# LN1 of tiles 6 to 15 transposed by DMA instead of TensorE, normalised three tiles ahead, with the weight loads behind the transposes

## The chip, the core and the metric

The kernel runs on one core of one Trainium2 chip. The metric is the device time of one execution in microseconds (us). Inside the core five engines follow their own instruction streams in order and meet at semaphores: TensorE (PE, with its weight loads shown apart as PEld), VectorE (DVE), ScalarE (ACT), GpSimd (POOL) and SyncE (SP). In this kernel SP issues all DMAs, so its stream is also the order of the one DMA queue.

## The reference

One transformer block of 2048 tokens and width 512 in bf16, with linear attention of 32 heads of 16 columns and a feed-forward part of width 1792:

```
x  = A_x                                   # 2048 x 512
q, k, v = split(layernorm(x) @ wqkv)       # 32 heads of 16
phi(t) = where(t > 0, t + 1, exp(t)) + 1e-6
kv = sum_s phi(k)[s] v[s]^T ;  z = sum_s phi(k)[s]
o  = phi(q) kv / (phi(q) . z + 1e-6)
h  = x + o @ wo
out = h + relu(layernorm(h) @ w1) @ w2
```

`B_x` is not used. The layernorms have no weights.

## The kernel before

The 2048 rows are 16 tiles of 128 rows (`NT`), and four chunks of four tiles (`CT`, 512 rows). The weights and all of x stay in SBUF. No scheduler orders the work (`manual_schedule`): each engine executes its instructions in the order in which the Python code issues them, and the semaphores alone are set automatically.

The kernel has two parts. **The key loop** (lines 313 to 330) goes over the 16 tiles and is what the change touches. **The rest** (from line 333) computes z, the small matrices of the heads and wo, the queries, h, the second layernorm and the feed-forward part, chunk by chunk. The second layernorm of chunks 1 to 3 is transposed by DMA already (`ln2_norm`, line 452).

In the key loop a tile t goes through these steps; the short names are the code's:

- `A_S(t)`, here **S(t)**: DVE takes the statistics of x (`st`, line 175, and `mv`, line 176). When the group of t is complete, ACT computes 1/sqrt(var + eps) as a Ln and an Exp (`rstd`, lines 169 and 170). Tiles 0 to 3 are groups of one, and the others are pairs: (4, 5), (6, 7), (8, 9) and so on. S of an odd tile is thus followed by the two small ACT instructions, and the norms of both tiles wait for them.
- `A_N(t)`, here **N(t)**: DVE writes the normalised tile `ln` (line 179).
- `A_T(t)`, here **T(t)**: four TensorE transposes of 128x128 into PSUM (line 187), and one ACT copy to `lnT` (line 193).
- `A_K(t)`, here **K(t)**: four matmuls, `lnT` by the key weights into `kps` (line 294).
- `phi_act(t)`: ACT reads `kps` and writes `e` = exp (line 199), and for some tiles also `r` = relu (line 203).
- `phi_dve(t)`: DVE clips `e` (line 208) and then adds, as `r + e` where ACT made the relu (`pk_all`, line 212), or as max(kps, 0) + e straight from PSUM where it did not (line 214).
- `A_G(t)`, here **G(t)**: four matmuls, `ln` by `pk_all`, accumulate the 512x512 matrix `gps` (line 301).

Iteration i issues T(i+1), K(i), G(i-1), phi_act(i), N(i+2), S(i+4), phi_dve(i), with S(3) and S(4), S(5) in iterations 0 and 1. TensorE thus repeats transposes, K and G, 12 instructions an iteration, and G(i-1) is the one that needs what DVE made last. Iterations 14 and 15 also hold a group of four query matmuls each (`q_group`, line 326), which need `wq_sb`.

SP issues x and the key weights first (lines 83 to 92), and then `wq`, `wv`, `wo`, `w1` and `w2` as five whole loads (lines 93 to 97). All of that is issued in the first 13.0 us, and SP's next work are the transposes of line 452. The first use of `wq` is at 36.7 us, of `wv` at 45.3 us, of `wo` at 48.1 us, and of `w1` at 61.9 us.

Of the kernel before, what the change touches and what calls it, by code (L numbers as in the profile page):

```python
# [11 lines left out]
BF16 = mybir.dt.bfloat16  # L12
# [4 lines left out]
def kernel(  # L17
# [13 lines left out]
    nc = tc.nc  # L31
    P = 128
    xf = A_x.flatten_outer_dims()
    of = out.flatten_outer_dims()
    S, D = xf.shape
# [3 lines left out]
    NT = S // P  # L39
    CW = 512  # L40
    CT = CW // P
# [6 lines left out]
    work = ctx.enter_context(tc.tile_pool(name="work", bufs=2))  # L48
# [7 lines left out]
    wqkv_v = A_wqkv.rearrange("(k p) n -> p k n", p=P)  # L56

    x_nat = big.tile([P, NT, D], BF16, name="x_nat")
    wq_sb = const.tile([P, KD, D], BF16, name="wq_sb")
    wk_sb = const.tile([P, KD, D], BF16, name="wk_sb")  # L60
    wv_sb = const.tile([P, KD, D], BF16, name="wv_sb")
    wo_sb = const.tile([P, KD, D], BF16, name="wo_sb")
    w1_sb = const.tile([P, KD, FF], BF16, name="w1_sb")
    w2_sb = const.tile([P, KF, D], BF16, name="w2_sb")
# [3 lines left out]
        name=nc.get_next_instruction_name(),  # L68
# [6 lines left out]
    def load_x(t0, n):  # L75
        nc.sync.dma_start(out=x_nat[:, t0 : t0 + n, :], in_=x_v[:, t0 : t0 + n, :])

    def load_wk(h):
# [11 lines left out]
    load_x(6, 2)  # L90
    load_x(8, 4)
    load_x(12, 4)
    nc.sync.dma_start(out=wq_sb[:], in_=wqkv_v[:, :, 0:D])
    nc.sync.dma_start(out=wv_sb[:], in_=wqkv_v[:, :, 2 * D : 3 * D])
    nc.sync.dma_start(out=wo_sb[:], in_=A_wo.rearrange("(k p) n -> p k n", p=P))
    nc.sync.dma_start(out=w1_sb[:], in_=B_w1.rearrange("(k p) n -> p k n", p=P))
    nc.sync.dma_start(out=w2_sb[:], in_=B_w2.rearrange("(k p) n -> p k n", p=P))


    eps5 = const.tile([P, 1], F32, name="eps5")  # L100
# [13 lines left out]
        out=mask3, in_=mask3, pattern=[[-DH, P // DH], [0, DH]],  # L114
# [3 lines left out]
        out=mask3, in_=mask3, pattern=[[DH, P // DH], [0, DH]],  # L118
# [8 lines left out]
        out=mask_h[:], in_=mask_h[:], pattern=[[P, KD], [-DH, H]],  # L127
# [3 lines left out]
        out=mask_h[:], in_=mask_h[:], pattern=[[-P, KD], [DH, H]],  # L131
# [4 lines left out]
        out=erep[:], in_=erep[:], pattern=[[1, D]],  # L136
# [3 lines left out]
        out=erep[:], in_=erep[:], pattern=[[-1, D]],  # L140
# [5 lines left out]
    lnT_c = [big.tile([P, KD, CW], BF16, name=f"lnT{c}") for c in range(NCH)]  # L146
# [20 lines left out]
    def rstd_of(mv, n):  # L167
        rstd = work.tile([P, n], F32, name="rstd", tag=f"rstd{n}", bufs=4)
        nc.scalar.activation(out=rstd[:], in_=mv[:, :, 1], func=ACT.Ln, bias=eps5[:], scale=1.0)
        nc.scalar.activation(out=rstd[:], in_=rstd[:], func=ACT.Exp, scale=-0.5)  # L170
        return rstd

    def stats(mv, k, src):
        st = work.tile([P, nc.vector.BN_STATS_DIM], F32, name="st", tag="st", bufs=4)
        nc.vector.bn_stats(out=st[:], in_=src)  # L175
        nc.vector.bn_aggr(out=mv[:, k, :], in_=st[:])  # L176

    def norm(dst, src, mv, rstd, k):
        nc.vector.tensor_scalar(  # L179
            out=dst, in0=src, scalar1=mv[:, k, 0:1], scalar2=rstd[:, k : k + 1],  # L180
            op0=ALU.subtract, op1=ALU.mult,
        )
# [7 lines left out]
    def evac_T(dst3, tp, on_act, k=KD):  # L190
        src3 = tp.rearrange("p (k n) -> p k n", k=k)
        if on_act:
            nc.scalar.activation(out=dst3, in_=src3, func=ACT.Copy)  # L193
        else:
            nc.vector.tensor_copy(out=dst3, in_=src3)

    def phi_act(ps, relu_on_act):
        e = work.tile([P, CW], BF16, name="e", tag="e", bufs=4)
        nc.scalar.activation(out=e[:], in_=ps, func=ACT.Exp)  # L199
        r = None  # L200
        if relu_on_act:
            r = work.tile([P, CW], BF16, name="r", tag="r", bufs=4)
            nc.scalar.activation(out=r[:], in_=ps, func=ACT.Relu)
        return e, r

    def phi_dve(ps, dst, er):
        e, r = er
        nc.vector.tensor_scalar(  # L208
            out=e[:], in0=e[:], scalar1=1.0, scalar2=1e-6, op0=ALU.min, op1=ALU.add
        )  # L210
        if r is not None:
            nc.vector.tensor_tensor(out=dst, in0=r[:], in1=e[:], op=ALU.add)
        else:
            nc.vector.scalar_tensor_tensor(  # L214
                out=dst, in0=ps, scalar=0.0, in1=e[:], op0=ALU.max, op1=ALU.add
            )
# [16 lines left out]
    def tick():  # L233
        due = [x for x in later if x[0] <= 0]
        later[:] = [x for x in later if x[0] > 0]
        for x in later:
            x[0] -= 1
        for _, fn in due:
            fn()
# [5 lines left out]
    def q_group(c, jq, relu_on_act):  # L245
        qps = q_mm(c, jq)
        er = phi_act(qps[:], relu_on_act)
        after(0, lambda: phi_dve(qps[:], pqT_c[c][:, jq, :], er))
# [6 lines left out]
    mvs, rstds, lns, tps, kpss, ers = {}, {}, {}, {}, {}, {}  # L255

    def A_S(t):
        g, k = where[t]
        if k == 0:
            mvs[g[0]] = work.tile(  # L260
                [P, len(g), nc.vector.BN_AGGR_DIM], F32, name="mv", tag=f"mv{len(g)}", bufs=4
            )
        stats(mvs[g[0]], k, x_nat[:, t, :])
        if k == len(g) - 1:
            rstds[g[0]] = rstd_of(mvs[g[0]], len(g))

    def A_N(t):
        g, k = where[t]
        lns[t] = work.tile([P, D], BF16, name="ln", tag="ln", bufs=6)
        norm(lns[t][:], x_nat[:, t, :], mvs[g[0]], rstds[g[0]], k)  # L270

    def A_first():

        lns[0] = work.tile([P, D], BF16, name="ln", tag="ln", bufs=6)
        for k in range(0, KD, 2):
            cols = slice(k * P, (k + 2) * P)
            norm(lns[0][:, cols], x_nat[:, 0, cols], mvs[0], rstds[0], 0)
        for k in range(0, KD, 2):
            tp = psum.tile([P, 2 * P], BF16, name="tph", tag="mm")
            for i in range(2):  # L280
                nc.tensor.transpose(
                    tp[:, i * P : (i + 1) * P], lns[0][:, (k + i) * P : (k + i + 1) * P], ident[:]
                )
            evac_T(lnT_c[0][:, k : k + 2, 0:P], tp, on_act=True, k=2)

    def A_T(t):
        c, j = divmod(t, CT)
        evac_T(lnT_c[c][:, :, j * P : (j + 1) * P], transpose(lns[t]), on_act=True)

    def A_K(t):  # L290
        c, j = divmod(t, CT)
        kpss[t] = psum.tile([P, D], F32, name="kps", tag="mm")
        for kd in range(KD):
            nc.tensor.matmul(  # L294
                kpss[t][:], lhsT=lnT_c[c][:, kd, j * P : (j + 1) * P], rhs=wk_sb[:, kd, :],
                start=(kd == 0), stop=(kd == KD - 1),
            )

    def A_G(t):
        for kd in range(KD):  # L300
            nc.tensor.matmul(  # L301
                gps[kd][:], lhsT=lns[t][:, kd * P : (kd + 1) * P], rhs=pk_all[:, t, :],
                start=(t == 0), stop=(t == NT - 1),
            )

    ok = lambda t: 0 <= t < NT
    A_S(0)
    A_S(1)
    A_first()
    warm(1)  # L310
    A_N(1)
    A_S(2)
    for i in range(NT):
        if ok(i + 1):
            A_T(i + 1)
        A_K(i)
        if ok(i - 1):
            A_G(i - 1)
        ers[i] = phi_act(kpss[i][:], relu_on_act=(i % 3 != 2))
        if ok(i + 2):  # L320
            A_N(i + 2)
        t = {0: 3, 1: 4}.get(i, i + 4)
        if ok(t):
            A_S(t)
        if i >= NT - 2:
            q_group(0, i - (NT - 2), False)
        phi_dve(kpss[i][:], pk_all[:, i, :], ers[i])
        if i == 1:
            A_S(5)
        tick()  # L330


# [276 lines left out]
```

## Time and profile before

| what | us |
|---|---|
| time, median of 3 runs (182.0 to 182.14) | 182.02 |
| span of the profiled execution, first to last instruction | 180.3 |
| median time less that span | 1.7 |
| PE busy in the span | 170.8 |
| DVE busy in the span | 110.4 |
| ACT busy in the span | 80.9 |
| first K to the last G of the key loop on PE | 6.0 to 43.9 |

The profile is of one execution. Its page states the span alone and no device time of its own; the median of the runs is 1.7 us longer. A line of the timeline gives the start and the length of an instruction or of a merged row of equal ones, its engine and line, what it writes and reads, and in brackets how long the engine idled before it and what released it. A table by stage gives the busy time of each engine in a stretch of the span. Granted TensorE clock is 1.00 in every stretch of the span. A PE row ends when its last result is out of the array, so that a row of four matmuls of 512 columns shows 1.03 us, while the next row can start 0.865 us after it; starts are what can be compared.

### The profile page before, as it was taken

The numbers are of one execution on the slowest core, as the hardware profiler recorded it, in microseconds if no ns is written. First come the engines' busy times: TensorE is split into PE (matmuls) and PEld (weight loads), VectorE is DVE, ScalarE is ACT, GpSimd is POOL, SyncE is SP. The second block draws the span as 40 slices with busy tenths as digits, with TensorE's granted clock in tenths as the row PEclk, the third lists the DMA queues.
The fourth block names the chain that finished last, engine by engine and source line by source line (L and its number), as shares of the span: only waits on it lengthen the run. The fifth ranks groups of instructions, "written<-read, shape, count | busy, mean of one in ns | idle before, by whom it ended". The sixth has DMA issues, their size and how long they took to land.

```text
span 180.3 us, 2413 instructions
## 1 busy us (share of the span) xinstructions
PE 170.8 (95%) x899; PEld 80.1 (44%) x916; DVE 110.4 (61%) x247; ACT 80.9 (45%) x162; POOL 4.0 (2%) x15
## 2 busy tenths in 40 slices
PE   7778999999999999999999999999999999999992
PEld 2334555546444444444444344444444444444461
DVE  3889999556799866988223788433498713343220
ACT  3768888856674998323007722003932100332000
POOL 7100000000000000000000000000000000000000
PEclk9999999999999999999999999999999999999999
DMA  5999970000000000002410000431000250000011
GB/s 139 291 331 378 377 232 4 0 0 4 0 4 0 0 0 0 2 4 58 111 35 29 0 4 0 87 87 58 0 0 4 40 135 29 29 0 4 29 58 31
DMA packets 15627, 11.69 MB, mean 65 GB/s; under 512 B 7040, under 2 KB 15104, under 8 KB 15616
## 3 DMA queue, kind: packets, MB, share of 16 engines
q1 hardware_dynamic: 15616, 11.54, 21.1%
q8 instruction: 7, 0.11, 0.2%
q14 instruction: 4, 0.03, 0.1%
HBM read 7.86 MB, written 2.10 MB: 55 GB/s over the span
## 4 chain that ended last, share of the span: by engine, by line
PE 70%; DVE 18%; ACT 6%; issue 2%; DMA 1%; DVEq 0%
PE fps L489 22%; PE pps L475 20%; PE gps L301 7%; PE kps L294 6%; DVE st L175 5%; PE qps L221 5%; PE hps L419 5%; DVE at L482 2%; PE fpsh L489 2%; DVE hn L179 2%; DVE mv L176 2%; DVE h_nat L443 1%; ACT lden L406 1%; ACT rden L408 1%; PE tp L187 1%
## 5 line engine op out<-in xcount | busy, mean ns | idle before, releaser
L475 PE MATMUL pps<-lnT,w_sb 128*128 128x512 bf16 x220 | 53.0, 379 | 0.8 <-ACT lnT L193 0.4
L489 PE MATMUL fps<-w_sb,at 128*128 128x512 bf16 x205 | 46.1, 379 | 0.6 <-DVE at L482 0.4
L480 ACT ACTIVATE at<-pps 128x512 bf16<-128x512 f32 x28 | 16.6, 595 | 60.6 <-PE pps L475 60.6
L489 PEld LDWEIGHTS <-at 128*128 128x128 bf16 x238 | 23.1, 98 | 26.2 <-DVE at L482 1.3
L475 PEld LDWEIGHTS <-w_sb 128*128 128x128 bf16 x224 | 21.9, 98 | 27.3 <-issue 1.7
L497 DVE TENSOR_TENSOR o_t<-fps,h_nat 128x512 bf16<-128x512 f32 x15 | 10.4, 692 | 29.1 <-PE fps L489 29.1
L482 DVE TENSOR_SCALAR at<-pps 128x512 bf16<-128x512 f32 x28 | 19.0, 680 | 9.3 <-PE pps L475 9.3
L301 PE MATMUL gps<-pk_all,ln 128*128 128x512 bf16 x61 | 15.9, 379 | 1.0 <-DVE pk_all L214 0.5
L419 PE MATMUL hps<-m_sb,pqs 128*128 128x512 bf16 x63 | 16.6, 379 | 0.1
L294 PE MATMUL kps<-wk_sb,lnT 128*128 128x512 bf16 x62 | 16.3, 379 | 0.1
L221 PE MATMUL qps<-lnT,wq_sb 128*128 128x512 bf16 x62 | 15.7, 379 | 0.2
L175 DVE BATCH_NORM_STATS2 st<-x_nat 128x6 f32<-128x512 bf16 x16 | 11.0, 685 | 1.8 <-DMA x_nat<-in_A_x_dram 1.7
L208 DVE TENSOR_SCALAR e<-e 128x512 bf16<-128x512 bf16 x32 | 8.9, 278 | 4.7 <-ACT e L199 4.7
L199 ACT ACTIVATE e<-qps 128x512 bf16<-128x512 f32 x16 | 9.4, 600 | 4.6 <-PE qps L221 4.6
L175 DVE BATCH_NORM_STATS2 st<-h_nat 128x6 f32<-128x512 bf16 x16 | 11.0, 689 | 0.4
L410 DVE TENSOR_TENSOR pqs<-pqT,rden 128x512 bf16<-128x512 bf16 x12 | 5.1, 426 | 9.1 <-ACT rden L408 9.0
L199 ACT ACTIVATE e<-kps 128x512 bf16<-128x512 f32 x16 | 9.5, 595 | 2.5 <-PE kps L294 2.5
L193 ACT ACTIVATE lnT<-tp 128x512 bf16<-128x512 bf16 x17 | 10.0, 590 | 0.5 <-PE tp L187 0.5
L419 PEld LDWEIGHTS <-pqs 128*128 128x128 bf16 x64 | 6.2, 98 | 8.4 <-DVE pqs L410 1.2
L301 PEld LDWEIGHTS <-ln 128*128 128x128 bf16 x64 | 6.2, 97 | 8.5 <-issue 1.4
L221 PEld LDWEIGHTS <-wq_sb 128*128 128x128 bf16 x64 | 6.0, 98 | 7.2 <-issue 0.8
L443 DVE TENSOR_TENSOR h_nat<-hps,x_nat 128x512 bf16<-128x512 f32 x12 | 8.2, 686 | 0.9 <-PE hps L419 0.8
(72 smaller groups left out, 134.9 us busy)
## 6 DMA issues: line engine op xcount, KB each, us to landing
w_sb<-in_B_w_dram SPq DMA_DIRECT2D x2, 1792.0 KB, 14.0
out_dram<-o_t SPq DMA_DIRECT2D x15, 128.0 KB, 1.7
x_nat<-in_A_x_dram SPq DMA_DIRECT2D x2, 512.0 KB, 7.3
x_nat<-in_A_x_dram SPq DMA_DIRECT2D x4, 128.0 KB, 2.2
wk_sb<-in_A_wqkv_dram SPq DMA_DIRECT2D x2, 256.0 KB, 3.7
x_nat<-in_A_x_dram SPq DMA_DIRECT2D x2, 256.0 KB, 4.7
wq_sb<-in_A_wqkv_dram SPq DMA_DIRECT2D x1, 512.0 KB, 8.7
wv_sb<-in_A_wqkv_dram SPq DMA_DIRECT2D x1, 512.0 KB, 9.4
```

The source lines that it names most:

```text
L175: nc.vector.bn_stats(out=st[:], in_=src)
L199: nc.scalar.activation(out=e[:], in_=ps, func=ACT.Exp)
L221: nc.tensor.matmul(qps[:], lhsT=wq_sb[:, kd, jq * P : (jq + 1) * P], rhs=lnT_c[c][:, kd, :], start=(kd == 0), stop=(kd == KD - 1),)
L294: nc.tensor.matmul(kpss[t][:], lhsT=lnT_c[c][:, kd, j * P : (j + 1) * P], rhs=wk_sb[:, kd, :], start=(kd == 0), stop=(kd == KD - 1),)
L301: nc.tensor.matmul(gps[kd][:], lhsT=lns[t][:, kd * P : (kd + 1) * P], rhs=pk_all[:, t, :], start=(t == 0), stop=(t == NT - 1),)
L419: nc.tensor.matmul(hps[:], lhsT=pqss[c][jb][:, j * P : (j + 1) * P], rhs=m_sb[:, jb, :], start=(jb == 0), stop=(jb == KD - 1 and c > 0),)
L443: nc.vector.tensor_tensor(out=h_nat[:, t, :], in0=hps[:], in1=x_nat[:, t, :], op=ALU.add)
L475: nc.tensor.matmul(pps[:], lhsT=w1_sb[:, kd, f * P : (f + 1) * P], rhs=hnT_c[c][:, kd, :], start=(kd == 0), stop=(kd == KD - 1),)
L480: nc.scalar.activation(out=acts[c][:, f, :], in_=pps[:], func=ACT.Relu)
L482: nc.vector.tensor_scalar(out=acts[c][:, f, :], in0=pps[:], scalar1=0.0, scalar2=None, op0=ALU.max)
L489: nc.tensor.matmul(fps[:], lhsT=acts[c][:, f, j * P : (j + 1) * P], rhs=w2_sb[:, f, n0:n1], start=(f == 0), stop=(f == KF - 1),)
L497: nc.vector.tensor_tensor(out=o_t[:], in0=fps[:], in1=h_nat[:, t, n0:n1], op=ALU.add)
```

## The change

- T(6) to T(15) are gone from TensorE, and with each the ACT copy to `lnT`. In their place N(t) is followed by one DMA transpose from SBUF to SBUF, which SP issues.
- The loads of `wq`, `wv` and `wo` are cut into halves of two of four row blocks. One half is issued behind each of the transposes 6 to 11. `w1` and `w2` are issued whole behind transpose 15.
- From iteration 5 on, N is three tiles ahead (it was two) and S five tiles ahead (it was four). The catching up is in iteration 4, which issues N(6), N(7), S(8), phi_dve(4), S(9), in this order. Iterations 0 to 3 are as before, and so are the transposes on TensorE up to T(5), in iteration 4.
- ACT computes the relu of all tiles except 2 (before, DVE did it from PSUM for 2, 5, 8, 11 and 14).
- `ln` has 8 buffers (it had 6).

The rest of the kernel is not changed.

```diff
-    nc.sync.dma_start(out=wq_sb[:], in_=wqkv_v[:, :, 0:D])
-    nc.sync.dma_start(out=wv_sb[:], in_=wqkv_v[:, :, 2 * D : 3 * D])
-    nc.sync.dma_start(out=wo_sb[:], in_=A_wo.rearrange("(k p) n -> p k n", p=P))
-    nc.sync.dma_start(out=w1_sb[:], in_=B_w1.rearrange("(k p) n -> p k n", p=P))
-    nc.sync.dma_start(out=w2_sb[:], in_=B_w2.rearrange("(k p) n -> p k n", p=P))
+    wo_v = A_wo.rearrange("(k p) n -> p k n", p=P)
+    w1_v = B_w1.rearrange("(k p) n -> p k n", p=P)
+    w2_v = B_w2.rearrange("(k p) n -> p k n", p=P)
+
+    def load_half(dst, src, h):
+        nc.sync.dma_start(out=dst[:, 2 * h : 2 * h + 2, :], in_=src[:, 2 * h : 2 * h + 2, :])
+
+    wq_v, wv_v = wqkv_v[:, :, 0:D], wqkv_v[:, :, 2 * D : 3 * D]
...
+    TD = 6
+    beside = {6: (wq_sb, wq_v, 0), 7: (wq_sb, wq_v, 1), 8: (wv_sb, wv_v, 0), 9: (wv_sb, wv_v, 1),
+              10: (wo_sb, wo_v, 0), 11: (wo_sb, wo_v, 1)}
+
     def A_N(t):
         g, k = where[t]
-        lns[t] = work.tile([P, D], BF16, name="ln", tag="ln", bufs=6)
+        lns[t] = work.tile([P, D], BF16, name="ln", tag="ln", bufs=8)
         norm(lns[t][:], x_nat[:, t, :], mvs[g[0]], rstds[g[0]], k)
+        if t >= TD:
+            c, j = divmod(t, CT)
+            nc.sync.dma_start_transpose(out=lnT_c[c][:, :, j * P : (j + 1) * P], in_=lns[t][:])
+            if t in beside:
+                load_half(*beside[t])
+            if t == NT - 1:
+                nc.sync.dma_start(out=w1_sb[:], in_=w1_v)
+                nc.sync.dma_start(out=w2_sb[:], in_=w2_v)
...
+    S_at = {0: [3], 1: [4, 5], 2: [6], 3: [7], 4: [8, 9]}
+    N_at = {0: [2], 1: [3], 2: [4], 3: [5], 4: [6, 7]}
...
     for i in range(NT):
-        if ok(i + 1):
+        if ok(i + 1) and i + 1 < TD:
             A_T(i + 1)
         A_K(i)
         if ok(i - 1):
             A_G(i - 1)
-        ers[i] = phi_act(kpss[i][:], relu_on_act=(i % 3 != 2))
-        if ok(i + 2):
-            A_N(i + 2)
-        t = {0: 3, 1: 4}.get(i, i + 4)
-        if ok(t):
+        ers[i] = phi_act(kpss[i][:], relu_on_act=(i != 2))
+        for t in N_at.get(i, [i + 3]):
+            if ok(t):
+                A_N(t)
+        ss = [t for t in S_at.get(i, [i + 5]) if ok(t)]
+        for t in ss[:1]:
             A_S(t)
         if i >= NT - 2:
             q_group(0, i - (NT - 2), False)
         phi_dve(kpss[i][:], pk_all[:, i, :], ers[i])
-        if i == 1:
-            A_S(5)
+        for t in ss[1:]:
+            A_S(t)
         tick()
```

More of the change, by code (lines that the diff above doesn't have):

```diff
@@ L265, in A_S @@
             rstds[g[0]] = rstd_of(mvs[g[0]], len(g))
+    TD = 6
+    beside = {6: (wq_sb, wq_v, 0), 7: (wq_sb, wq_v, 1), 8: (wv_sb, wv_v, 0), 9: (wv_sb, wv_v, 1),
+              10: (wo_sb, wo_v, 0), 11: (wo_sb, wo_v, 1)}
     def A_N(t):
         g, k = where[t]
-        lns[t] = work.tile([P, D], BF16, name="ln", tag="ln", bufs=6)
+        lns[t] = work.tile([P, D], BF16, name="ln", tag="ln", bufs=8)
         norm(lns[t][:], x_nat[:, t, :], mvs[g[0]], rstds[g[0]], k)
+        if t >= TD:
[6 more added lines that the diff above has]
+                nc.sync.dma_start(out=w2_sb[:], in_=w2_v)
     def A_first():
-        lns[0] = work.tile([P, D], BF16, name="ln", tag="ln", bufs=6)
+        lns[0] = work.tile([P, D], BF16, name="ln", tag="ln", bufs=8)
         for k in range(0, KD, 2):
```

## The prediction, made before the changed kernel was run

> **What bounds the kernel now.** I read the page first, then the key loop, the only stage that the change touches, by a table of one row per iteration, then VectorE's timeline.
>
> ```profile
> span 180.3 us, 2413 instructions
> PE 170.8 (95%) x899; PEld 80.1 (44%) x916; DVE 110.4 (61%) x247; ACT 80.9 (45%) x162; POOL 4.0 (2%) x15
> ```
>
> The page says TensorE (PE), at 95%, and VectorE (DVE) at 61%. That is an average. In the key loop, with the stretches cut at the starts of G (so 18.52 is the start of G(4), 20.47 of G(5)), and the columns PE, weight loads, DVE, ACT:
>
> ```profile
> 16.57:18.52 1.95, 1.95 (x13) 1.00 (x12) 1.76 (x6) 1.88 (x4) 0.00 (x0) 1.00 1.02 401
> 18.52:20.47 1.95, 1.95 (x13) 1.00 (x12) 1.88 (x6) 1.54 (x4) 0.00 (x0) 1.00 1.03 395
> 28.30:30.25 1.95, 1.95 (x14) 1.01 (x13) 1.77 (x6) 1.88 (x4) 0.00 (x0) 1.00 0.00 0
> ```
>
> PE is never free here, and DVE is nearly full too: its remaining 0.1 to 0.2 us are mostly the gaps between dependent instructions, as the timeline of one iteration shows:
>
> ```profile
> 16.34 0.41 DVE L179 TENSOR_SCALAR ln<-x_nat,mv,rstd 128x512 bf16<-128x512 bf16 x1
> 16.66 0.68 DVE L175 BATCH_NORM_STATS2 st<-x_nat 128x6 f32<-128x512 bf16 x1
> 17.38 0.18 DVE L176 BATCH_NORM_AGGREGATE mv<-st 128x2 f32<-128x6 f32 x1
> 17.48 0.26 DVE L208 TENSOR_SCALAR e<-e 128x512 bf16<-128x512 bf16 x1
> 17.89 0.42 DVE L212 TENSOR_TENSOR pk_all<-r,e 128x512 bf16<-128x512 bf16 x1 [0.15 <-ACT r L203]
> 18.23 0.41 DVE L179 TENSOR_SCALAR ln<-x_nat,mv,rstd 128x512 bf16<-128x512 bf16 x1
> ```
>
> From start to start: N to S 0.32, `st` to `mv` 0.72, `mv` to `e` 0.10, `e` to `pk_all` 0.36 (15.63 to 15.99 one iteration earlier; here 0.41, held up by ACT), `pk_all` to the next N 0.35. The sum is **1.85 us**, where ACT makes the relu. Where DVE makes it (tile 5: `e` 19.38, `pk_all` 19.68, next N 20.29) the last two terms are 0.30 and 0.61 in place of 0.36 and 0.35, so 2.05. PE needs 1.95 for transposes, K and G. DVE is therefore the next bound, 0.1 us behind the present one. The rows to price the change from:
>
> ```profile
> L187 PE MATMUL tp<-ident,ln 128*128 128x128 bf16 x60 | 5.8, 219 | 1.1 <-DVE ln L179 1.1
> lnT<-hn SPq DMA_TRANSPOSE x12, 2.4
> wk_sb<-in_A_wqkv_dram SPq DMA_DIRECT2D x2, 256.0 KB, 3.7
> 81.89 5.23 SPq L452 DMA_TRANSPOSE lnT<-hn  x4
> 11.65 0.18 DVE L176 BATCH_NORM_AGGREGATE mv<-st 128x2 f32<-128x6 f32 x1
> 12.44 0.41 DVE L179 TENSOR_SCALAR ln<-x_nat,mv,rstd 128x512 bf16<-128x512 bf16 x1 [0.60 <-ACT rstd L170]
> ```
>
> **What the change takes from PE.** In the chain of waits four transposes of a tile take 0.222 us, and K and G 0.865 each: 1.95. Ten tiles lose them: 10 x 0.222 = 2.2 us of PE, if PE stays the bound at 1.73 an iteration. It does not.
>
> **A floor between K and G.** From the end of K(12)'s row (33.28 + 1.03 = 34.31) to the end of `pk_all` (35.47 + 0.42) are 1.58 us (exp, relu, add); G starts 0.05 later. K(i+1) starts 0.865 after G(i-1), its row lasts 1.03, and G(i+1) starts 1.63 behind it: 3.52 us for two iterations, 1.76 each. That is the pace where DVE is not the bound.
>
> **What DVE has to do, tile by tile.** Up to `pk_all` of tile 3 (start 15.99) the order is unchanged, and nothing there waits for a load but the first tile. From there, in the new order of DVE:
>
> - Iteration 4, N(6) N(7) S(8) phi(4): 0.35 to N(6), 0.33 to N(7) (estimate: the two `hn` norms at 57.30 take 0.70 together, 0.41 one), 0.32, 0.72, 0.10, 0.36 = 2.18. `pk_all` of 4 at 18.17, done 18.59, G(4) at **18.64** (18.52 before).
> - Then S(9), then N(8), which now needs the rstd of S(9) at once: **a new wait**. The row at 12.44 is its like: `mv` at 11.65, the Ln and Exp on ACT, N 0.79 later, with DVE idle for 0.60. On ACT the Ln stands ahead of the exp of tile 5, so that exp is held too, but it is done in time (about 20.5, and its relu 21.0). Sum: 0.34 to S(9), 0.72, 0.79 to N(8), 0.32 to S(10), 0.72, 0.10, 0.36 = 3.35. `pk_all` of 5 at 21.52, G(5) at **21.99** (20.47 before, so 1.52 late).
> - Iterations 6 to 10 hold N, S and phi each: 5 x 1.85 = 9.25. Here S of an odd tile comes before a phi, so its rstd has 0.81 us before the next N, against 0.79 needed: no further wait. `pk_all` of 10 at 30.77, G(10) at 30.77 + 0.42 + 0.05 = **31.24** (30.25 before, 0.99 late).
> - From iteration 11 on S is finished, and PE and the floor set the pace: G(11) 31.24 + 1.73 = 32.97; G(12) by the floor from K(12), which starts 31.24 + 0.865 = 32.105: 32.105 + 1.03 + 1.63 = 34.76; G(13) 36.49. Before, G(13) is at 36.10, so **0.39 us late**. Neither kernel has a T behind that, so from here the rest shifts as it is.
>
> The relus on ACT are in this sum: tiles 5 and 8 save DVE 0.20 each (2.05 to 1.85); 11 and 14 lie where DVE has time. ACT takes four relus of 0.59, and loses ten copies of 0.59 (line 193), so nothing there is late.
>
> **The transposes.** The issue takes SP 5.23 / 4 = 1.3 us, and a tile lands 2.4 us after its issue begins. A half load costs SP 0.48 (the halves of `wk`, 0.96 for two). A pair takes 1.78, less than DVE's 1.85, so SP follows N. SP is idle from 13.0 us to 81.9 before, so no other work waits behind. Transpose 6 starts with the end of N(6) at 16.8 and lands at 19.2; K(6) can start at 19.5. That is the tightest; were it late by up to 1.6 us, G(5) waits for DVE until 21.99 anyway. Transpose 7 starts at 18.6, lands at 21.0 (K(7) at 22.9); 9 at 22.3, 24.7 (K(9) 26.6); 11 at 26.0, 28.4 (K(11) 30.3). If each also waits for the half load ahead of it, add 0.7 us (256 KB at the 355 to 401 GB/s of the table's last column), which stays inside. I take no cost. The outer bound is 3.7 us for a half (the row of `wk`, which landed in a full queue): a pair of 1.2 + 3.7 = 4.9 from 16.8 lands transpose 11 at 16.8 + 5 x 4.9 + 2.4 = 43.7, 13.4 us late. The point from which it decides is a pair of 2.2 us. I choose the small end, as the new queue is nearly empty, like that of the row at 81.89.
>
> A rule speaks against this edit: the Trainium skill, VectorE: DVE Perf Modes, "The three transpose paths", gives 1309 ns to a 128x128 DMA transpose, 390 ns to one on TensorE, and advises TensorE where PSUM will do. An estimate from that page, four blocks in sequence, would be 5.2 us a tile, pairs of 5.7, and K(11) some 20 us late; the row above has all four blocks landed in 2.4.
>
> **The loads.** By the starts above, `wq` is issued by 20.4, `wv` by 24.1, `wo` by 27.8, `w1` and `w2` from about 34.5. Their uses are at 36.7, 45.3, 48.1, 61.9 and later, and `w1` and `w2` took 14.0 us: 48.5. All hidden; without that cover `w1` would have to be over 13 us later still. The 8 `ln` buffers suffice: tile t lives from N in iteration t-3 to G in t+1.
>
> **Sum.** 180.3 + 0.39 = 180.7 us of span; with the 1.7 outside, 182.02 + 0.39 = **182.4 us**, +0.21%. The measurement tells about 0.2% from no change, 0.36 us, so I stand at that edge.
>
> **The rivals.**
>
> - *PE keeps what it is given.* If the DVE group runs in 1.73 or less in place of 1.85 and the wait ahead of N(8) is filled, 2.2 us go: 179.8. For it: PE is busy in all of each iteration today, which the page shows and DVE's 61% does not contradict. Against: three cycles of 1.85 with nothing to wait for. It decides from a group under 1.76 us. Chance 0.10, with what lies on the way to it (179.8 to 181.6): faster.
> - *The wait ahead of N(8) costs nothing* (0.69 less in the sum, 0.79 against 0.10): 181.7; from 181.66 to 182.1. For it: the rstd needs two small instructions only. Against: the row at 12.44 with 0.60 idle. Chance 0.13: within 0.2%.
> - *The transposes are late*, as the half loads share their queue: a pair of 3 us would land transpose 11 at 34.2, 3.9 us late, 186.3; a pair of 2.3 some 0.5 us more than the forecast, 182.9. Chance 0.12, slower. For it: up to 3.7 us in the row of `wk`.
> - *The stretch costs DVE more*, by a second wait for rstd in iterations 7 and 9 (spare 0.02 us; up to 0.3 each): 182.8 to 183.4. Chance 0.10, slower.
> - *Forecast*, 182.1 to 182.8: chance 0.55, of which 0.33 lies above 182.38 (slower) and 0.22 below (within).
>
> Faster 0.10; within 0.13 + 0.22 = 0.35; slower 0.33 + 0.10 + 0.12 = 0.55. The range 181.4 to 183.8 leaves out most of the first rival and half of the third. It doesn't hold the outer bound of the transposes.
>
> **What would show it.** DVE idle for about 0.6 us ahead of N(8), released by ACT `rstd`; starts of G from 5 to 10 spaced at 1.85, with PE waiting for `pk_all` line by line; G(13) some 0.4 us later than at 36.10; no K waiting for a DMA but at most K(6); the rest after the loop unchanged in length. I am wrong if PE waits for `lnT` from a DMA beyond K(6), or if G comes at 1.73 to 1.76 before iteration 10.

## The result and the profile after

| kernel | median us (range) | span of the profiled execution |
|---|---|---|
| before | 182.08 (182.0 to 182.31, 4 runs) | 180.3 |
| after | 183.16 (183.0 to 183.35, 4 runs) | 181.2 |

The ratio is 1.0058, with a 95% interval of 1.0045 to 1.007: **slower by 1.1 us**. The forecast was 182.4, 0.4 slower. Direction and range hold; the size does not, and it is wrong in three terms of which two nearly cancel.

The page after, its span and its line of engines:

```profile
span 181.2 us, 2356 instructions
PE 169.8 (94%) x860; PEld 77.7 (43%) x876; DVE 109.6 (61%) x247; ACT 77.2 (43%) x156; POOL 4.0 (2%) x15
```

PE has 39 matmuls fewer in the records (40 were taken out), and is busy for 1.0 us less. (By the starts it has 2.2 us less to do, but a row that is followed by a wait counts its full 1.03 us.) The span is 0.8 longer. So PE waits more, and the table by iteration, cut at the new starts of G, says where. G(4) starts at 18.71, G(5) at 22.07, G(6) at 24.33 and so on; the columns are the length, PE, weight loads, DVE, ACT, POOL, clock, DMA share and GB/s:

```profile
18.71:22.07 3.36, 1.89 (x8) 0.77 (x8) 2.58 (x8) 2.45 (x6) 0.00 (x0) 1.00 0.58 144
22.07:24.33 2.26, 1.89 (x9) 0.78 (x8) 1.71 (x6) 0.84 (x3) 0.00 (x0) 1.00 0.87 238
24.33:26.75 2.42, 1.90 (x9) 0.70 (x9) 2.28 (x7) 0.75 (x2) 0.00 (x0) 1.00 0.67 88
...
30.47:32.32 1.85, 1.85 (x9) 0.78 (x8) 1.71 (x6) 1.51 (x4) 0.00 (x0) 1.00 0.77 202
```

Against the predicted lengths of 3.35, 1.85, 1.85 and 1.85 the first and the last hold, and two rows are too long: 2.26 (0.41 over) and 2.42 (0.57 over). DVE's timeline shows the first of these:

```profile
19.30 0.18 DVE L179 BATCH_NORM_AGGREGATE mv<-st 128x2 f32<-128x6 f32 x1
20.08 0.41 DVE L182 TENSOR_SCALAR ln<-x_nat,mv,rstd 128x512 bf16<-128x512 bf16 x1 [0.60 <-ACT rstd L173]
...
23.08 0.26 DVE L211 TENSOR_SCALAR e<-e 128x512 bf16<-128x512 bf16 x1
23.85 0.43 DVE L215 TENSOR_TENSOR pk_all<-r,e 128x512 bf16<-128x512 bf16 x1 [0.51 <-ACT rstd L173]
```

The first pair is the new wait ahead of N(8), as forecast: 0.78 from `mv` to N (0.79 forecast), with 0.60 idle. The second pair was not forecast: from `e` of tile 6 to its `pk_all` it takes 0.77, where tiles 4, 5, 7, 9 and 10 take 0.36. (Tiles 8 and 11 to 14 take 0.49, as they wait for `r`.) The view puts it down to `rstd`, but `pk_all` reads `r` and `e`, and ACT had written `r` by 22.0. A releaser that the instruction does not read is a guess of the view, to be tested (it is, below).

The second long row shows in PE's timeline of the changed kernel:

```profile
25.87 1.04 PE L309 MATMUL kps<-wk_sb,lnT 128*128 128x512 bf16 x4 [0.52 <-DMA lnT<-ln]
```

SP's queue of the same kernel, with the start and length of each issue:

```profile
20.77 1.19 SPq L280 DMA_TRANSPOSE lnT<-ln  x1
22.00 0.58 SPq L98 DMA_DIRECT2D wv_sb<-in_A_wqkv_dram  x1
22.68 2.44 SPq L280 DMA_TRANSPOSE lnT<-ln  x1
25.17 0.58 SPq L98 DMA_DIRECT2D wv_sb<-in_A_wqkv_dram  x1
```

K(8) waits for transpose 8, issued at 20.77 and landed at 25.83, 5.1 us later; K(9), at 27.79 in place of 27.61, waits for transpose 9. The issue of transpose 9 is stretched from 1.2 to 2.44. The four transposes without a half load behind them land 2.4 to 2.7 us after their issue, the other four with one 2.6 to 3.1. What is in the queues of the changed kernel from 20.7 to 25.5 us, with packets, MB and share of the 16 DMA engines:

```profile
q1 hardware_dynamic: 1971, 0.87, 78.2%
q8 instruction: 1, 0.02, 2.2%
q14 instruction: 1, 0.01, 2.1%
```

Beside the kernel's own transfers run two single packets of the kind "instruction": pieces of the engines' programs, of 16 and of 8 KB. The larger runs from 23.23 us for 1.69 us, the other from 24.91 for 1.64, in the middle of transposes 8 and 9. (Their times are counted from the span's start, here and below. Where an expectation names one, it was counted 0.3 us later.)

The last difference is at the end. All DMA that remains after 178.7 us in the profile of before, when the last output has landed:

```profile
q14 instruction: 1, 0.01, 1.3%
```

It comes at 180.09, and the program ends 1.93 us after the last output. After the change no such piece is left there (the last of its size is at 148.7), and the end follows the last output by 1.28: **0.65 us gained**, and by nothing that the change does to the work.

### The profile page after: what moved, and what is told of

Read it like the earlier page. It is cut to its first block, busy times and chain, and to the rows that moved or that the text cites. A ratio compares the mean times of both kernels' runs of the same rounds, so it can differ in the third digit from the quotient of the medians.

```text
span 181.2 us, 2356 instructions
## 1 busy us (share of the span) xinstructions
PE 169.8 (94%) x860; PEld 77.7 (43%) x876; DVE 109.6 (61%) x247; ACT 77.2 (43%) x156; POOL 4.0 (2%) x15
## 4 chain that ended last, share of the span: by engine, by line
PE 65%; DVE 21%; ACT 6%; DMA 4%; issue 2%; DVEq 0%
PE fps L507 22%; PE pps L493 20%; DVE st L178 7%; PE hps L437 5%; PE qps L224 5%; PE gps L316 4%; PE kps L309 4%; DMA lnT<-ln 3%; DVE at L500 2%; DVE mv L179 2%; DVE ln L182 2%; PE fpsh L507 2%; DVE hn L182 2%; DVE h_nat L461 1%; ACT lden L424 1%
## 5 line engine op out<-in xcount | busy, mean ns | idle before, releaser
L172 ACT ACTIVATE rstd<-mv,eps 128x2 f32<-128x2 f32 (+2 forms) x15 | 4.4, 296 | 10.9 <-DVE mv L179 10.9
L309 PEld LDWEIGHTS <-lnT 128*128 128x128 bf16 x64 | 5.9, 98 | 7.4 <-DMA lnT<-ln 1.7
```

The lines of the kernel that those rows point to most:

```text
L309: nc.tensor.matmul(kpss[t][:], lhsT=lnT_c[c][:, kd, j * P : (j + 1) * P], rhs=wk_sb[:, kd, :], start=(kd == 0), stop=(kd == KD - 1),)
```

## The experiments

The ratios below are to runs of before on the same chip, whose medians were 182.04 (first four experiments), 182.05 (next four) and 182.06 (last three). Each run has one profile. All runs with the new DMA transposes also have the shorter end, so 0.6 us of any comparison of their times with before does not come from the key loop.

**Does the wait ahead of N(8) cost what the sum says?** `e1_stats_first` takes both S of iteration 4 ahead of phi_dve(4), so that the rstd has phi's time to come.

```diff
-        for t in ss[:1]:
+        for t in ss if i == 4 else ss[:1]:
             A_S(t)
...
-        for t in ss[1:]:
+        for t in [] if i == 4 else ss[1:]:
```

> The changed kernel with S(9) moved ahead of phi_dve(4) in iteration 4, all else as it is. Theory DVE (the loss is VectorE's catching up): the wait for rstd ahead of N(8), 0.60 us, goes; N(8) follows pk_all of 4 at once, G(5) comes near 21.4 in place of 22.07, G(4) about 0.8 later than 18.71; the time falls by 0.6 to 0.7 from 183.16, to about 182.5. Theory DMA (the loss is the late landing of transposes 8 and 9): transpose 8 is issued when SP is through with the second half of wq, at 20.8 as before, so K(8) starts at 25.9 as before and the time stays at 183.1.

Measured: 182.99 us, ratio 1.0041 (1.0026 to 1.0056). The wait is gone: N(8) follows `pk_all` at once, and G(5) starts at 21.23 in place of 22.07. PE still waits for transpose 8:

```profile
25.19 1.04 PE L309 MATMUL kps<-wk_sb,lnT 128*128 128x512 bf16 x4 [0.67 <-DMA lnT<-ln]
```

N(8) is earlier, but SP, still busy with the transposes and halves before it, issues transpose 8 at 20.64 (20.77 in the changed kernel). In this profile it lands after 4.5 us in place of 5.1, and most of the gain is kept: G(13) is at 36.88, 0.69 earlier than in the changed kernel. But the profiled run is the fastest of its seven, 182.18 where the others have 182.8 to 183.1, so it shows a good case. The median falls by 0.2 alone. That the other runs lose the gain at the late transposes fits the second theory, but no profile of one of them was kept, so it is not shown.

**Is it the half loads?** `e2_loads_first` issues `wq`, `wv` and `wo` whole at the start, as before the change.

```diff
+    for dst, src in ((wq_sb, wq_v), (wv_sb, wv_v), (wo_sb, wo_v)):
+        nc.sync.dma_start(out=dst[:], in_=src)
...
-            if t in beside:
-                load_half(*beside[t])
```

> The changed kernel with wq, wv and wo loaded whole at the start as in the kernel before; the transposes then have the queue to themselves, w1 and w2 stay behind transpose 15. Theory DMA by the half loads: every transpose lands 2.4 to 2.6 us after its issue, no K waits for one, G(6) to G(10) are spaced at 1.85 us, G(13) comes at 36.5 in place of 37.57 and the time falls by 1.0, to about 182.1. Theory DMA by code fetches (16 KB of instructions through the same rings at 23.5 us): transpose 8 or 9 still lands more than 3.5 us after its issue, K(8) or K(9) still waits 0.3 us or more, and the time stays over 182.5.

Measured: 182.25, ratio 1.0009 (0.9999 to 1.0018). The piece of 16 KB comes at 22.87, near its old place, but it finds only transposes in the queue. The view of the tile `lnT` between 14 and 40 us, in the changed kernel:

```profile
DMA to landing us min/median/max: 2.4/2.8/5.1
```

The same view of `e2_loads_first`:

```profile
DMA to landing us min/median/max: 2.4/2.4/3.6
```

No K waits for a DMA (one weight load does, for 0.2), and the time falls by 0.9. Both theories were right in part: transpose 9 still lands 3.6 us after its issue, beside the piece, but inside the lead of three tiles. The late `pk_all` of tile 6 is still there (22.93 to 23.69).

**Does the stagger pay?** `e3_two_ahead` leaves N two and S four tiles ahead, as before the change; then there is no catching up and no wait for rstd.

```diff
-    S_at = {0: [3], 1: [4, 5], 2: [6], 3: [7], 4: [8, 9]}
-    N_at = {0: [2], 1: [3], 2: [4], 3: [5], 4: [6, 7]}
+    S_at = {0: [3], 1: [4, 5]}
+    N_at = {}
...
-        for t in N_at.get(i, [i + 3]):
+        for t in N_at.get(i, [i + 2]):
...
-        ss = [t for t in S_at.get(i, [i + 5]) if ok(t)]
+        ss = [t for t in S_at.get(i, [i + 4]) if ok(t)]
```

> The changed kernel without the catching up: N two tiles ahead and S four, the order of the kernel before; the transposes by DMA, the half loads and the relus on ScalarE stay. Theory DVE: no wait for rstd after iteration 2, pk_all is spaced at 1.85 us from tile 3 (15.99) on, G(10) comes at 29.4 (before 30.25, changed 32.32), G(13) at 34.7, and the time is 182.0 - 1.4 = 180.7; transposes land 0.1 to 0.4 us after PE could start K, which costs nothing at this pace. Theory DMA: with one tile less of lead K waits for nearly every transpose from 7 to 11, G is spaced at 2 us or more, and the time is 183.2 or above.

Measured: 183.56, ratio 1.0086 (1.0058 to 1.0115). The waits of PE from 17 to 36 us, in total, how often, and the longest:

```profile
PE kps L309 <- DMA lnT<-ln: 2.8, 3, 1.9
```

With two tiles of lead, late transposes reach K three times: 0.43 at K(7), 1.90 at K(8), 0.49 at K(12). (The expectation of `e6` below has the last as K(11).)

**What is the order alone worth?** `e4_order_only` keeps the new order of DVE and the relus on ACT, but transposes every tile on TensorE and loads all weights at the start.

```diff
-    TD = 6
+    TD = NT
```

> The changed order of N and S and the relus on ScalarE alone: all transposes on TensorE and all loads at the start, as in the kernel before. Theory DVE: the catching up costs what it costs in the changed kernel, G(5) at about 22.0 and G(10) at about 31.2, then 1.95 us an iteration, G(13) at 37.1, so the time is 182.0 + 1.0 = 183.0, slower than before though nothing goes through DMA. Theory DMA: as no tile is transposed by DMA, the time is that of the kernel before, 182.0 to 182.3.

Measured: 184.08, ratio 1.011 (1.0094 to 1.0126), twice the expected loss. PE's timeline of this kernel has a wait that I had left out, at K(6), but the G(5) behind it waits for DVE all the same:

```profile
20.48 1.04 PE L311 MATMUL kps<-wk_sb,lnT 128*128 128x512 bf16 x4 [0.62 <-ACT lnT L198]
21.96 1.02 PE L318 MATMUL gps<-pk_all,ln 128*128 128x512 bf16 x4 [0.44 <-DVE pk_all L217]
```

ACT's copy of tile 6 stands behind the `rstd` that waits for S(9), so K(6) is late, but G(5) is at 21.96, where it was expected (22.0). The loss that I had not expected comes behind it: `pk_all` of tile 6 is late here too (G(6) at 24.22), and PE, with transposes at 1.95 an iteration where the expectation took 1.85 up to G(10), can't catch up: G(10) at 32.02, G(13) at 37.87. In `e2_loads_first`, with the same order and the transposes by DMA, G(13) is at 36.81. The work taken from PE is thus worth 1.1 us here. The medians differ by 1.8, but 0.65 of that is the end of the program, which `e4` has as before has it.

**What is the late `pk_all`?** In the changed kernel, in `e1`, `e2` and `e4` it is late by the same 0.4 (as it is in `e8` below). It is the 64th instruction of DVE's program in each, counting the waits that are instructions of their own; and it is also the same tile in each. `e5_code_shift` is `e2_loads_first` with three small instructions more at the start of DVE's program, so that the 64th is another.

```diff
+    spare = const.tile([P, 3], F32, name="spare")
+    for n in range(3):
+        nc.vector.memset(spare[:, n : n + 1], 0.0)
```

> The run e2 (loads of wq, wv, wo first) with three more instructions at the start of VectorE's program, each a memset of one column that nothing reads. In all four runs with the new order pk_all of tile 6 came 0.77 us after e instead of 0.36; it is the 64th instruction of VectorE in each of them, while in the kernel before and in e3 that place holds mv, behind a st of 0.69 us. Theory code: VectorE is held up 0.4 us where its program passes that place; shifted by three, the place lies behind st again, and the delay goes: G(6) 1.85 after G(5), G(10) at 31.2 in place of 31.57, G(13) at 36.4 in place of 36.81, time 182.25 - 0.4 = 181.85. Theory wait: pk_all of 6 waits for the Exp of rstd (which ended 0.12 us before it in all four): then the delay stays at tile 6 and the time at 182.25.

Measured: 181.98, ratio 0.9997 (0.9986 to 1.0007), 0.27 below `e2_loads_first`. DVE's timeline:

```profile
22.84 0.18 DVE L184 BATCH_NORM_AGGREGATE mv<-st 128x2 f32<-128x6 f32 x1
22.93 0.26 DVE L216 TENSOR_SCALAR e<-e 128x512 bf16<-128x512 bf16 x1
23.30 0.43 DVE L220 TENSOR_TENSOR pk_all<-r,e 128x512 bf16<-128x512 bf16 x1
```

From `e` to `pk_all` 0.37, and in this kernel the Exp of `rstd` ends at 23.58, after `pk_all` has started. The `rstd` named in the profile of after was therefore not what it waited for. G(5) to G(13) are at 21.93, 23.78, 25.63, 27.48, 29.33, 31.18, 32.90, 34.70 and 36.42: within 0.08 of the predicted 21.99 to 36.49, every one. (Its G(0) is at 9.12, 0.10 earlier than before; counted from there, G(13) is 0.42 late, 0.39 predicted.) This kernel is the prediction's model, with the two disturbances gone.

**How much of the late transposes is the lead?** `e6_two_ahead_loads_first` joins the edits of `e3` and `e2`.

> The run e3 (N two tiles ahead, S four, as before) with wq, wv and wo loaded whole at the start, so that the transposes have the queue to themselves; w1 and w2 stay behind transpose 15. Theory DVE and queue: the waits of K(7), K(8) and K(11) for a DMA in e3 (0.43, 1.90, 0.49) came from the half loads; without them transposes land 2.4 us after issue, pk_all is spaced at 1.85 from tile 4 on, G(10) comes at 29.4 (before 30.25), G(13) at 34.75 (before 36.10), time 182.04 - 1.35 = 180.7. Theory lead: two tiles are too little lead for a transpose of 2.4 us; K waits 0.2 to 0.5 us for most of the ten, G comes at 2.0 us or more, time 182.0 or above.

Measured: 181.98, ratio 0.9987 (0.9977 to 0.9998). With no half loads in the queue, the pieces of code alone (here at 22.30 and 22.70) let transpose 8 land after 3.9 us, and the shorter lead shows it:

```profile
24.41 0.82 PE L309 MATMUL kps<-wk_sb,lnT 128*128 128x512 bf16 x3 [1.40 <-DMA lnT<-ln]
```

Neither theory named this: no other K waits, so in this profile two tiles of lead are enough but for the one late transpose.

**What are the relus worth?** `e7_relu_dve` is `e5_code_shift` with the relus divided as before (and a fourth small instruction, to keep the shift).

```diff
-        ers[i] = phi_act(kpss[i][:], relu_on_act=(i != 2))
+        ers[i] = phi_act(kpss[i][:], relu_on_act=(i % 3 != 2))
```

> The run e5 with the relu of tiles 5, 8, 11 and 14 on VectorE again, as in the kernel before (and four columns set at the start in place of three, to keep the place of the 64th instruction behind a st). Theory DVE: tiles 5 and 8 cost VectorE 0.20 us more each, G(10) comes 0.4 later than in e5, tiles 11 and 14 lie where VectorE has time; time 0.4 over e5, about 182.25. Rival (ScalarE is the bound of the loop): the time falls or stays, as ScalarE loses four relus of 0.59.

Measured: 182.26, ratio 1.0011 (1.0002 to 1.0019), 0.28 above `e5_code_shift`. G(10) is at 31.54 against 31.18: 0.18 for each of the tiles 5 and 8, 0.20 predicted. This profile also parts the two pieces: the 8 KB one comes at 20.53, beside transpose 8, which lands after 2.4 us as if alone; the 16 KB one at 23.14, beside transpose 9, which lands after 3.2.

**Is it the piece of code?** `e8_fetch_earlier` is the changed kernel with one warm-up block less and 16 small matmuls more ahead of the loop. If the piece belongs to TensorE's program, it comes earlier.

```diff
-    warm(9)
+    warm(8)
+    for _ in range(16):
+        nc.tensor.matmul(gps[3][:, 0:1], lhsT=zeros[:, 0:P], rhs=zeros[:, 0:1], start=True, stop=True)
```

> The changed kernel with one of the nine first warm-up matmuls replaced by 16 of one column, which makes TensorE's program 30 instructions longer ahead of the key loop. TensorE's code is fetched by the DMA rings in pieces of 16 KB (256 instructions); in the changed kernel one of them falls at 23.5 us, beside the half loads and transposes 8 and 9, which land 5.1 us after issue. Theory fetch (the piece of code holds one ring back 1.7 us and the transposes behind it): the piece falls about two iterations earlier, at 19.8 us, and the late landing moves with it: transposes 8 and 9 land within 3.2 us, 6 or 7 lands later than 2.9, K(8) and K(9) don't wait and the time falls by 0.4 to 0.7, to about 182.6. Theory backlog (the queue runs full, as each pair of transpose and half load needs more than the interval): transposes 8 and 9 land over 4.5 us after issue as in the changed kernel, time 183.1.

Measured: 182.23, ratio 1.0016 (1.0006 to 1.0026): 0.9 below the changed kernel, half loads and all. That is more than the 0.4 to 0.7 expected. The piece comes at 17.74 in place of 23.23 (19.5 expected), with 30 instructions more in TensorE's program ahead of it. It now meets transpose 6, which lands after 3.8 us in place of 2.6, as PE's timeline shows:

```profile
20.57 1.04 PE L311 MATMUL kps<-wk_sb,lnT 128*128 128x512 bf16 x4 [0.93 <-DMA lnT<-ln]
21.98 0.81 PE L318 MATMUL gps<-pk_all,ln 128*128 128x512 bf16 x3 [0.36 <-DVE pk_all L217]
```

K(6) waits 0.93, but G(5) would have waited for DVE until 21.98 anyway: the wait for rstd covers it, as the prediction said of K(6). Transpose 8 lands after 2.9 us and transpose 9 after 3.6, over the 3.2 expected, with the 8 KB piece beside it (at 24.99). K(8) and K(9) wait for nothing.

**A version that beats both.** `e9_two_ahead_fetch_earlier` is `e6` with the piece moved further ahead, to 16.29, ahead of all transposes.

```diff
-    warm(9)
+    warm(7)
+    for _ in range(24):
+        nc.tensor.matmul(gps[3][:, 0:1], lhsT=zeros[:, 0:P], rhs=zeros[:, 0:1], start=True, stop=True)
```

> The run e6 (transposes by DMA, N two tiles ahead, wq, wv and wo first) with two of the nine first warm-up matmuls replaced by 24 of one column: TensorE's program is 44 instructions longer ahead of the key loop, so that the piece of its code fetched at 22.6 us in e6, beside transpose 8 (3.9 us to landing, K(8) waits 1.40), falls ahead of transpose 6, at about 15 us. Theory fetch: transpose 8 lands within 2.6 us, K(8) waits less than 0.1, G(7) comes 1.85 after G(6), G(13) at 34.8 to 35.0 in place of 36.26 (before 36.10), time 181.98 - 1.3 = 180.6 to 180.8. Rival lead: K(8) waits all the same, as two tiles of lead are too few, time 181.7 or above.

Measured: **180.83**, ratio 0.9931 (0.991 to 0.9952), 1.2 below before and 2.3 below the changed kernel. Its waits of PE from 17 to 38 us:

```profile
PE kps L311 <- DMA lnT<-ln: 0.2, 1, 0.2
```

All transposes land in 2.4 to 2.7. G(4) to G(13) go from 18.33 to 35.15 (34.8 to 35.0 expected), 0.95 earlier than before at the end. The pace is DVE's 1.85 up to G(7), and 1.89 on average up to G(10), with the 0.2 at K(9). The span is 1.6 shorter than before: 0.95 of that is the key loop, and 0.6 the end of the program (1.30 us behind the last output, 1.93 before), which a kernel without the transposes can have too, as the next run shows. The six runs lie in two groups, 180.25 to 180.47 and 181.2 to 181.35; I have one profile (of 180.47) and don't know what sets them apart.

**Is the gain at the end the length of a program?** `e10_before_longer_sp` is the kernel before with `wv`, `wo`, `w1` and `w2` in 19 pieces in place of 4, so that SP has 100 instructions in the trace in place of 85 (the changed kernel has 108). Same bytes, same order, nothing else.

```diff
+    for dst, src, n in pieces:
+        for k in range(0, src.shape[1], n):
+            nc.sync.dma_start(out=dst[:, k : k + n, :], in_=src[:, k : k + n, :])
```

> The kernel before with wv, wo, w1 and w2 loaded in 19 pieces in place of four, which makes SP's program 15 instructions longer and changes nothing else. From the end of the last output transfer to the end of the program there are 1.93 us in the kernel before and 1.95 in e4 (both without new transposes; a piece of code of 8 KB is fetched by the DMA rings in that time), and 1.27 to 1.31 in the changed kernel and in seven runs with DMA transposes (the last such piece is fetched at 149 us). Theory code at the end: SP's longer program has that piece fetched earlier; from the last transfer to the end 1.3 us, time 182.05 - 0.65 = 181.4, G(13) at 36.1 as before. Rival: the shorter end has to do with the transposes themselves; then the time stays at 182.05.

Measured: 181.53, ratio 0.9974 (0.9966 to 0.9983). The piece at the end is gone, and the end comes 1.43 us after the last output in place of 1.93. The key loop is as before (G(13) at 36.01). So a tuned kernel gains 0.5 us by more instructions on an idle engine. Nine of the twelve runs have the gain (181.45 to 181.58); three, at 181.93 to 182.09, do not, and no profile of those was kept.

**Can DVE's group be made shorter?** `e11_phi_fused` is `e9` with `e`'s clip and the addition in one instruction (it leaves out the added 1e-6 of those tiles' keys).

```diff
-        nc.vector.tensor_scalar(out=e[:], in0=e[:], scalar1=1.0, scalar2=1e-6, op0=ALU.min, op1=ALU.add)
...
-            nc.vector.tensor_tensor(out=dst, in0=r[:], in1=e[:], op=ALU.add)
+            nc.vector.scalar_tensor_tensor(out=dst, in0=e[:], scalar=1.0, in1=r[:], op0=ALU.min, op1=ALU.add)
```

> The run e9 with clip and add of the keys in one VectorE instruction, min(e, 1) + r, for all tiles but 2; it leaves out the 1e-6 that the reference adds to phi of the keys (and of those queries whose relu ScalarE makes). Theory DVE: if the fused one takes 0.43 like the add, N, S and phi take 1.50 us in place of 1.85, if it takes 0.69 like the one from PSUM, 1.75; in both cases the floor between K and G (1.76) and the DMA's lead set the pace from tile 4: G(10) at 28.6 to 28.8 in place of 29.4, G(13) 34.0 to 34.3, time 0.5 to 0.7 under e9. Rival: with the shorter interval K waits for transposes by as much, and the time is that of e9.

Measured: 181.59, ratio 0.9974 (0.9957 to 0.9992), 0.8 above `e9`. The runs again lie in two groups, 181.0 to 181.2 and 182.0 to 182.2, each 0.8 to 0.9 above the like group of `e9`. G(13) is at 35.97, where 34.0 to 34.3 was expected. A miss. The group of the fused instruction, with its count, busy time, mean ns and the idle time before it:

```profile
L216 DVE SCALAR_TENSOR_TENSOR pk_all<-e,r 128x512 bf16<-128x512 bf16 x15 | 10.3, 688 | 4.3 <-ACT r L210 3.6
```

It takes 688 ns, as long as the two it replaces (about 0.28 and 0.43), and since it needs `r` where the clip needed only `e`, it also starts later: 3.6 us of waits for ACT in 15 tiles.

## Why the prediction was right in sign and short in size

The sum, by G(13), the last point before the rest: forecast 0.39 late, measured 1.47 late. The lines on PE's timeline, before and after:

```profile
36.10 1.03 PE L301 MATMUL gps<-pk_all,ln 128*128 128x512 bf16 x4
37.57 1.02 PE L316 MATMUL gps<-pk_all,ln 128*128 128x512 bf16 x4
```

The terms, as after minus before. The first, third and fourth are differences of the time from G(0) to G(13), which is 26.88 before, 27.30 in `e5`, 27.69 in `e2` and 28.29 after:

| term | predicted us | measured us | shown by |
|---|---|---|---|
| the order of DVE, with the wait ahead of N(8), and catching up from G(10) on | 0.39 | 0.42 | `e5` less before |
| the key loop starts later | 0 | 0.06 | G(0) at 9.28 against 9.22 |
| late `pk_all` of tile 6 | 0 | 0.39 | row 22.07; `e2` less `e5` |
| late transposes 8 and 9 | 0 | 0.60 | row 24.33; after less `e2`; gone in `e8` too |
| end of the program | 0 | -0.65 | last output to end; `e4`, `e10` |

0.42 + 0.06 + 0.39 + 0.60 = 1.47 to G(13), and 1.47 - 0.65 = 0.82, against 0.83 between the two spans. The medians differ by 1.08, since the profiled run of after is the lowest of its four (183.0 against 183.16) and what lies outside the span is 0.1 more (1.84 against 1.7).

That the time lies inside the forecast range is luck in part: without the shorter end, which was not foreseen, it would be about 183.8, the upper edge. By the prediction's own sign, PE waiting for `lnT` from a DMA beyond K(6), its account of the transposes was wrong.

- **What bounds the kernel, and the pace of 1.85.** Right. Taking 2.2 us from PE gave a pace set by DVE, 1.85 until G(10), and then 1.72 and 1.80; `e5` shows it in each row. The rival in which PE keeps the 2.2 us is refuted even where almost nothing is late (G(13) is 0.95 earlier in `e9`).
- **The wait ahead of N(8).** Right in size (0.78 from `mv` to N against 0.79). The rival that it costs nothing is refuted by G(5). `e1` takes the wait away, and G(5) comes 0.84 earlier; its median gains 0.2 alone, and where the rest is lost is not shown.
- **The relus.** Right: 0.18 a tile against 0.20.
- **"I take no cost" for the transposes, and "SP follows N".** This is the step that failed, by 0.60. The pair of transpose and half load cost SP 1.91 (1.78 forecast), a little over DVE's 1.85, and the transpose landed inside its lead in four of six pairs. What I left out is a third user of the queues, the engines' programs. `e2` (no halves: no K waits), `e8` (halves kept, piece moved: none left at K(8)) and `e6` (no halves, shorter lead: 1.40) show that it takes the pieces together with either the halves or a short lead. The rival "the transposes are late" had the right place and a wrong cause (a pair of 2.3 or more throughout); the delay is a single one.
- **"No further wait" in iterations 6 to 10.** Failed by 0.4, at tile 6. The rival "the stretch costs DVE more" named a second wait for rstd; `e5` shows it is not that. It is tied to a place in DVE's program, and what happens there no run shows. In the kernel before the 64th instruction is an `mv` behind an `st` of 0.69 us, which is long enough to cover a hold-up of 0.4; that it does is not shown.
- **"The rest after the loop unchanged in length".** Failed by 0.65 us to the good. Without it the change would have cost some 1.7. That the piece at the end is SP's is argued from the counts (85 instructions with it in before and `e4`, 100 to 108 without it in the others); `e10` shows that it goes when SP's program gets longer. Why the end then comes earlier is open: the piece starts 1.69 us behind the last output before, when the other kernels have already ended, and 1.98 us behind it in `e4`, after that kernel's own last instruction.

How a piece of code holds up a transpose (one ring stopped, say, while the transpose needs all of them) is not shown; the runs show that the delay moves with the larger piece. What each piece does by itself can be read where they lie apart. Without half loads the 16 KB piece made it 3.2 us to landing (`e7`), the 8 KB piece 2.4 (`e7`) and 2.7 (`e9`). With half loads the 16 KB piece made it 3.8 in place of 2.6 (transpose 6 in `e8`), and the 8 KB piece 3.6 in place of 2.9 (transpose 9 in `e8`). In the changed kernel the two came one behind the other, and it was 5.1. The Trainium skill, Runtime: NRT & Kernel Launch, "Instruction fetch mechanics", says that programs are fetched in blocks of 16 KiB while the engine runs, at a cost that is mostly hidden. The trace agrees as to the block for TensorE's pieces (16 KB each; the others are of 8 KB) and as to the engine that fetches (the view of PE's waits names data alone). It is the transposes beside it that pay: they land 0.8 us (`e7`) to 1.5 us (`e6`) later without half loads, and 2.2 us later with them (5.1 against 2.9).

## What to carry to other kernels

Where a path is taken off one engine, follow every iteration to the next bound: here 0.22 us of PE an iteration were worth 0.1, since DVE stood right behind, and a single catch-up iteration ate what that gave. A wait that you fill moves the stop to the next thing that was just in time, so check the lead of each transfer before counting a gain. And when a transfer lands late once and not again, look at the kinds of the DMA queues for pieces of the program: some small instructions ahead of the loop can move such a piece to a place where nothing waits.

## What the runs showed of the hardware that was not expected

- A 16 KB piece of TensorE's program, 1.0 to 1.7 us in the queue, and an 8 KB piece near it delayed a DMA transpose in flight from 2.4 us to 3.6 and 3.9 (`e2`, `e6`), and to 5.1 with half loads in the queue. Sixteen tiny matmuls moved the larger piece from 23.2 to 17.7 us, for 0.9 us of time.
- Where a program's last fetch lay at its very end (before, `e4`), the end came 0.65 us later behind the last output than where it did not (after). With 15 more SP instructions (`e10`) the fetch was gone from there, and the time 0.5 us shorter in the median, though not in three of its twelve runs.
- An instruction of DVE came 0.4 us late, at one place of its program in five kernels (after, `e1`, `e2`, `e4`, `e8`), and not where three or four more instructions stood ahead (`e5`, `e7`).
- `scalar_tensor_tensor` on 128x512 in bf16 from SBUF takes 0.69 us, where `tensor_tensor` takes 0.43 and `tensor_scalar` 0.26 to 0.28 on the same data.
- With no loads beside them, DMA transposes of 128x512 from SBUF to SBUF landed 2.4 to 2.7 us after their issue, all ten of them (`e9`).
